# Decay attention and a highway FFN: k and q turned in halves of 64 rows, q loaded eight tokens to a row

## The chip, the cores and the metric

The kernel runs on one core of a Trainium2 chip. The metric is device time in microseconds. Engines are named as the profile names them: PE (matrix multiply, with PEld for its weight loads), DVE, ACT and POOL (elementwise engines), SP (which here only issues transfers). All times below are microseconds unless marked ns.

## The reference

Inputs are q, k and v of shape (4, 8, 768, 64), that is four batches, eight heads, 768 tokens and 64 channels, a decay `lam` per head, and the weights of a highway layer.

```python
for b in range(nb):                       # blocks of 64 tokens
    intra = einsum('bhic,bhjc->bhij', qb, kb) * Dmask      # lam^(i-j), causal
    out   = einsum('bhij,bhjd->bhid', intra, vb)
    out  += einsum('bhid,bhde->bhie', qb * lam_pow, kv_state)
    kv_state = lam_block * kv_state + einsum('bhsd,bhse->bhde', kb * rev_pow, vb)
x = out, heads side by side               # (3072 tokens, 512)
H = relu(x @ w_h);  T = sigmoid(x @ w_t + b_t)
return T * H + (1 - T) * x
```

The kernel computes the same in blocks of 128 tokens with the decay put into q (as lam to the token's number) and into v (as its inverse), so the mask is plain ones and zeros and the state needs no factor.

## The kernel before, in words

The 3072 tokens are cut into 12 steps n of 256 tokens, three to a batch; each step has two blocks b of 128 tokens, one on each half of the 128 partitions. One partition holds two neighbouring tokens (J = 2), so a load of k, q or v is made of runs of 512 bytes. Each step has six loads of 256 KB (`Lk`, `Lq`, `Lv`, each in two halves of four heads); the weights come as four transfers of 512 KB (`W`).

The order of everything is written out by hand in one list, `PLAN`. A token is an operation with its step, the engine after `@` and the PSUM banks after `=`; each engine runs its tokens in the list's order. For a step:

- `CK`, `CQ`, `CV` cast k to bf16, and scale q and v by the decay into bf16 (mostly on POOL).
- `TK`, `TQ` turn k and q on PE, eight transposes of 128x128 each, each into one bank (L204); `EK`, `EQ` copy the two banks to SBUF (128x1024, on ACT or DVE).
- `SS` computes scores of one head parity and, between them, the update of the state kv (L216 and L221; 64x64 tiles of the array). `S` and `U` are the same two apart, for step 0. `KE` copies the state (tile ss).
- `M` multiplies the scores by the mask `tri` on DVE (L255, tile m).
- `I` starts the output o from state times q (L271, 128x128 tiles); `A` adds masked scores times v (L281, 64x64 tiles).
- `D` copies o from PSUM to xT in bf16, the FFN's input (L101 on ACT, L103 on DVE).
- `F` is a block of eight FFN matmuls of 256 columns (L300, result bh for w_h, bt for w_t; the names F.n.u.w carry w as the last number); `H`, `G`, `X` are relu and subtract (tile hm, DVE), sigmoid (ACT, in place) and the gate (tile th, DVE). The last step is done as two groups of 128 columns, 11 and 12.
- `R` turns xT and th back and adds them: 32 matmuls of 64 rows, 128 columns and 64 moving columns, the row halves in turn, into two banks (L347, result bx; for the last step L327 with 128 rows); `E` copies the result to o and `ST` stores it.
- `Z` are matmuls on zeros in the start (bspin, L366); `WC` casts the weights; `B` and `BC` bring the bias into place.

Loads and stores are all issued by SP in the list's order. The transfers share eight semaphores in turn, so one waits for the eighth last.

The lines that the change rewrites most, the turns and the taking of o:

```python
for j in range(J):
    T.transpose(t[:, i, j, :], get(x + "b", n)[:, j, h:h + 2, :], id128)
...
copy(eng, xT[...].rearrange("p n (q j) -> p n j q", j=J),      # writes every second element
     get("o", n, b).rearrange("p n (j q) -> p n j q", j=J))
```

Of the kernel before, what the change touches and what calls it, by code (L numbers as in the profile page):

```python
# [17 lines left out]
Lk.0.0 Lv.0.1 Lv.0.0 Lq.0.0 Lk.0.1 Lq.0.1 Lv.1.1 CK.0.0@POOL Lq.1.0 Z.12=0 TK.0.0=0 Lq.1.1 CV.0.0@DVE Lk.1.0  # L18
CQ.0.0@POOL EK.0.0@DVE Lv.1.0 CV.0.1@DVE CK.0.1@ACT Lk.1.1 Z.11=1 TQ.0.0=1 B=2 EQ.0.0@ACT CQ.0.1@POOL W.0.1 W.0.0
Z.6=0 TQ.0.1=3 TK.0.1=4 EQ.0.1@DVE U.0.0 EK.0.1@ACT W.1.1 S.0.0=56 KE.0.0@DVE S.0.1=01 CQ.1.2@POOL W.1.0 M.0.0.1 Z.1=3  # L20
U.0.1 I.0=34 M.0.1.1 KE.0.1@ACT Lk.2.1 M.0.0.0 A.0.1 M.0.1.0 TQ.1.2=0 Lq.2.1 CV.1.2@DVE CK.1.2@ACT EQ.1.2@ACT Lq.2.0
Z.8=1 TK.1.2=1 A.0.0 EK.1.2@DVE Lk.2.0 D.0.0@DVE Z.3=5 SS.1.1=56 WC.0.0.1@ACT WC.0.0.0@POOL M.1.1.0 KE.1.0@ACT
WC.0.1.0@POOL D.0.1@ACT Lv.2.1 WC.0.1.1@DVE Z.4=0 SS.1.0=01 M.1.1.1 I.1=35 KE.1.1@ACT Lv.2.0 F.0.0.0=4 WC.1.1.0@DVE PT
M.1.0.1 Lk.3.1 F.0.1.0=6 M.1.0.0 WC.1.0.0@POOL WC.1.0.1@ACT Lk.3.0 WC.1.1.1@DVE A.1.1 A.1.0 BC F.0.0.1=1 H.0.1 Lq.3.1
D.1.1@ACT H.0.0 D.1.0@ACT F.0.1.1=0 Lq.3.0 CQ.2.2@POOL F.1.0.0=2 Lv.3.0 G.0.1@ACT CK.2.2@DVE F.1.0.1=6 Lv.3.1
G.0.0@ACT X.0.1@DVE TQ.2.2=5 Lq.4.0 X.0.0@DVE TK.2.2=4 EQ.2.2@ACT CV.2.2@POOL F.1.1.0=3 Lq.4.1 EK.2.2@DVE G.1.0@ACT
H.1.0 SS.2.0=01 Lk.4.1 H.1.1 CK.3.2@POOL SS.2.1=54 Lk.4.0 M.2.0.1 F.1.1.1=2 KE.2.0@ACT M.2.1.0 Lv.4.0 TK.3.2=3 M.2.1.1
CQ.3.2@POOL G.1.1@ACT I.2=15 M.2.0.0 Lv.4.1 A.2.1 X.1.0@DVE A.2.0 Lk.5.0 R.0=40 D.2.0@ACT D.2.1@DVE CV.3.2@POOL
TQ.3.2=6 E.0.0@ACT Lk.5.1 F.2.1.1=1 E.0.1@ACT EQ.3.2@DVE Lq.5.1 EK.3.2@ACT X.1.1@DVE F.2.1.0=5 CQ.4.2@POOL Lq.5.0
R.1=40 H.2.1 SS.3.1=62 Lv.5.0 F.2.0.0=3 CK.4.2@POOL KE.3.0@ACT M.3.1.1 Lv.5.1 E.1.1@ACT M.3.1.0 SS.3.0=52 E.1.0@ACT  # L30
H.2.0 Lq.6.0 TQ.4.2=0 KE.3.1@ACT CV.4.2@POOL M.3.0.1 TK.4.2=6 G.2.1@ACT Lq.6.1 F.2.0.1=4 M.3.0.0 EQ.4.2@ACT EK.4.2@DVE
Lv.6.0 I.3=32 A.3.0 CK.5.2@POOL A.3.1 Lk.6.1 SS.4.1=56 D.3.0@ACT D.3.1@DVE TK.5.2=0 KE.4.0@ACT M.4.1.1 Lk.6.0
F.3.0.0=2 G.2.0@ACT CQ.5.2@POOL EK.5.2@DVE Lv.6.1 SS.4.0=36 H.3.0 F.3.0.1=0 Lq.8.0 M.4.0.0 CV.5.2@POOL M.4.0.1
TQ.5.2=2 Lk.9.0 G.3.0@ACT F.3.1.0=3 X.2.1@DVE Lq.7.0 EQ.5.2@ACT X.2.0@DVE F.3.1.1=6 CQ.6.2@POOL M.4.1.0 Lq.7.1
KE.4.1@ACT I.4=14 H.3.1 G.3.1@ACT R.2=25 Lk.8.1 X.3.0@DVE A.4.0 E.2.1@ACT X.3.1@DVE A.4.1 Lk.7.1 SS.5.0=30 E.2.0@ACT
D.4.0@DVE CK.6.2@POOL SS.5.1=56 D.4.1@ACT Lk.7.0 TQ.6.2=2 M.5.0.0 KE.5.0@ACT CV.6.2@POOL TK.6.2=1 M.5.1.1 Lv.7.0
EQ.6.2@ACT F.4.1.0=4 M.5.0.1 Lv.7.1 EK.6.2@ACT F.4.0.0=3 H.4.1 Lk.8.0 M.5.1.0 I.5=62 SS.6.1=01 H.4.0 Lq.8.1 A.5.0
KE.6.0@ACT M.6.1.0 CQ.7.2@POOL R.3=45 Lv.9.1 A.5.1 M.6.1.1 SS.6.0=30 D.5.0@ACT Lv.8.0 F.4.0.1=1 M.6.0.0 D.5.1@ACT
M.6.0.1 Lk.9.1 TQ.7.2=6 G.4.0@ACT CK.7.2@POOL F.5.0.0=3 Lq.10.1 EQ.7.2@ACT F.4.1.1=2 H.5.0 Lk.10.1 E.3.1@ACT X.4.0@DVE
TK.7.2=0 CV.7.2@POOL G.4.1@ACT I.6=63 ST.0 KE.6.1@DVE F.5.0.1=5 X.4.1@DVE Lv.8.1 F.5.1.0=1 G.5.0@ACT CK.8.2@POOL  # L40
EK.7.2@DVE Lq.9.0 A.6.0 E.3.0@ACT H.5.1 A.6.1 SS.7.1=20 Lq.9.1 D.6.0@ACT D.6.1@DVE TK.8.2=4 M.7.1.1 F.6.1.0=1 Lv.9.0
EK.8.2@ACT X.5.0@DVE CK.9.2@POOL F.6.1.1=6 KE.7.0@DVE Lk.10.0 CQ.8.2@POOL H.6.1 R.4=30 SS.7.0=54 Lk.11.1 E.4.0@ACT
F.5.1.1=1 E.4.1@ACT M.7.0.1 G.6.1@ACT ST.4 M.7.1.0 TK.9.2=3 Lq.10.0 M.7.0.0 TQ.8.2=0 G.5.1@ACT CV.8.2@POOL F.6.0.0=4
EQ.8.2@DVE Lk.11.0 KE.7.1@ACT X.5.1@DVE I.7=25 EK.9.2@ACT Lq.11.0 A.7.0 H.6.0 A.7.1 CQ.9.2@POOL SS.8.0=01 X.6.1@DVE
D.7.1@ACT Lv.10.1 SS.8.1=34 M.8.0.1 D.7.0@ACT F.6.0.1=6 KE.8.0@DVE Lq.11.1 CK.10.2@POOL F.7.0.0=5 M.8.1.0 G.6.0@ACT
M.8.1.1 ST.3 TQ.9.2=1 CV.9.2@POOL H.7.0 F.7.1.0=2 EQ.9.2@ACT Lv.10.0 X.6.0@DVE TK.10.2=3 M.8.0.0 ST.1 I.8=45
EK.10.2@ACT CQ.10.2@POOL H.7.1 SS.9.1=61 A.8.1 KE.9.0@ACT M.9.1.0 A.8.0 R.5=02 M.9.1.1 SS.9.0=36 CK.11.2@POOL
E.5.1@DVE F.7.0.1=1 KE.9.1@ACT M.9.0.1 E.5.0@ACT F.7.1.1=2 D.8.0@DVE D.8.1@ACT ST.5 CQ.11.2@POOL M.9.0.0 G.7.0@ACT
Lv.11.1 TK.11.2=6 Lv.11.0 I.9=04 F.8.1.0=5 EK.11.2@ACT ST.2 X.7.0@DVE TQ.10.2=3 G.7.1@ACT H.8.1 CV.10.2@POOL F.8.0.0=1
EQ.10.2@ACT R.6=65 H.8.0 A.9.1 X.7.1@DVE A.9.0 SS.10.1=31 D.9.0@ACT D.9.1@DVE F.8.1.1=2 E.6.1@ACT M.10.1.1 F.9.1.0=0  # L50
E.6.0@DVE G.8.1@ACT M.10.1.0 ST.6 TQ.11.2=4 CV.11.2@POOL KE.10.0@DVE F.9.1.1=5 EQ.11.2@ACT X.8.1@DVE SS.10.0=16
G.9.1@ACT H.9.1 R.7=32 M.10.0.1 KE.10.1@ACT F.8.0.1=4 X.9.1@DVE E.7.0@ACT M.10.0.0 E.7.1@ACT I.10=06 SS.11.0=53
G.8.0@ACT ST.7 A.10.0 M.11.0.0 A.10.1 SS.11.1=21 D.10.1@ACT X.8.0@DVE F.9.0.0=5 KE.11.0@ACT M.11.1.0 D.10.0@ACT
# [12 lines left out]
def kernel(  # L66
# [13 lines left out]
    C = 128  # L80
# [4 lines left out]
    J = 2  # L85
    N = B * NST
# [12 lines left out]
    def copy(eng, dst, src):  # L99
        if eng == "ACT":  # L100
            A.activation(dst, src, AF.Copy)  # L101
        else:
            ENG[eng].tensor_copy(dst, src)  # L103


    lam_bc = singles.tile([128, H], F32)
    A.dma_start(out=lam_bc, in_=lam.partition_broadcast(128))
    bt_r = singles.tile([KC, 128], F32)
    A.dma_start(out=bt_r, in_=moe_b_t.rearrange("(j p) -> j p", p=128))
    id128 = singles.tile([128, 128], BF16)  # L110
    make_identity(nc, id128)
    blank = singles.tile([128, 512], BF16)
# [53 lines left out]


    SRC = {"k": k, "q": q, "v": v}

    def load(x, n, p, eng):  # L170
        b, c = divmod(n, NST)
        hs = heads(p)
# [246 lines left out]
```

## Time and profile before

| | |
|---|---|
| median of 8 runs | 109.35 (108.67 to 110.16) |
| the profiled execution | 108.67, with a span of 106.8 and a mean PE clock of 0.991 of full speed |
| busy in the span | PE 100.0, DVE 82.4, ACT 71.8, POOL 55.6 |
| first F (L300) starts, last one ends | 22.1, 101.6 |
| moved | 20.98 MB read, 6.29 MB written; SP's queue 88.7% of 16 engines' span |
| eight transposes of 128x128 (L204) | 0.45 on the chain |
| xT<-bo, 128x512 | 750 ns on ACT (16), 728 ns on DVE (8) |
| ss<-kv, 128x512 | 596 ns on ACT (15), 680 ns on DVE (5) |
| qb, vs 128x1024 on POOL | 1902 ns each |

The busy time of PE counts modelled ends of matmuls, which overlap; the time a block takes on PE is read from the start of one block to the start of the next, which the chain of waits shows. Up to 13 us the program waits for its first loads; then the steps follow each other, a few in flight at a time; from about 95 only the FFN of the last steps and the stores are left.

### The profile page before, as it was taken

The numbers are of one execution on the slowest core, as the hardware profiler recorded it, in microseconds if no ns is written. First come the engines' busy times: TensorE is split into PE (matmuls) and PEld (weight loads), VectorE is DVE, ScalarE is ACT, GpSimd is POOL, SyncE is SP. The second block draws the span as 40 slices with busy tenths as digits, with TensorE's granted clock in tenths as the row PEclk, the third lists the DMA queues.
The fourth block names the chain that finished last, engine by engine and source line by source line (L and its number), as shares of the span: only waits on it lengthen the run. The fifth ranks groups of instructions, "written<-read, shape, count | busy, mean of one in ns | idle before, by whom it ended". The sixth has DMA issues, their size and how long they took to land.

```text
span 106.8 us, 4970 instructions
## 1 busy us (share of the span) xinstructions
PE 100.0 (94%) x2190; PEld 80.9 (76%) x2190; DVE 82.4 (77%) x140; ACT 71.8 (67%) x129; POOL 55.6 (52%) x46
## 2 busy tenths in 40 slices
PE   4997999999999999999999999999999999999950
PEld 1343655488987888899889888989898888889930
DVE  1053495879799687999995996999977998858860
ACT  2213244786875678599769776987697797587940
POOL 7028340427889987988368394999870700000000
PEclk9999999999999999999999999999999999999996
DMA  2799999999999999999999999999969335008264
GB/s 36 190 307 291 291 354 386 328 291 262 295 298 295 294 292 288 289 298 289 290 281 302 303 350 299 335 314 333 332 211 339 117 145 196 6 6 327 72 247 146
DMA packets 42701, 27.59 MB, mean 258 GB/s; under 512 B 1588, under 2 KB 38712, under 8 KB 42680
## 3 DMA queue, kind: packets, MB, share of 16 engines
q1 hardware_dynamic: 42528, 27.27, 88.7%
q8 instruction: 17, 0.28, 1.1%
q14 instruction: 4, 0.03, 0.1%
q10 hardware_dynamic: 152, 0.01, 0.1%
HBM read 20.98 MB, written 6.29 MB: 255 GB/s over the span
## 4 chain that ended last, share of the span: by engine, by line
PE 79%; DVE 6%; DMA 5%; issue 2%; POOL 1%; SPq 1%; ACT 1%; POOLq 0%; DVEq 0%
PE bt L300 19%; PE bh L300 18%; PE bs L216 8%; PE bo L281 7%; PE bx L347 6%; PE bqtr L204 6%; DMA qf<-in_q_dram 5%; PE bktr L204 5%; PE bspin L366 5%; PE bo L271 4%; DVE m L255 4%; PE kv L221 2%; POOL qb L190 1%; DVE hm L305 1%; SPq L173 1%
## 5 line engine op out<-in xcount | busy, mean ns | idle before, releaser
L300 PEld LDWEIGHTS <-w_b 128*128 128x128 bf16 x416 | 36.4, 98 | 4.6
L255 DVE TENSOR_TENSOR m<-bs,tri 128x512 bf16<-128x512 f32 x48 | 31.0, 680 | 2.2 <-PE bs L216 1.9
L190 POOL TENSOR_TENSOR qb<-qf,pow_q 128x1024 bf16<-128x1024 f32 (+1 forms) x13 | 23.5, 1811 | 9.3 <-DMA qf<-in_q_dram 9.1
L314 ACT ACTIVATE bt<-bt,bt_col 128x256 f32<-128x256 f32 (+1 forms) x52 | 22.0, 432 | 5.7 <-PE bt L300 2.9
L300 PE MATMUL bh<-xT,w_b 128*128 128x256 bf16 (+1 forms) x208 | 25.0, 265 | 0.0
L300 PE MATMUL bt<-xT,w_b 128*128 128x256 bf16 (+1 forms) x208 | 24.5, 265 | 0.0
L190 POOL TENSOR_TENSOR vs<-vf,pow_v 128x1024 bf16<-128x1024 f32 x10 | 19.0, 1902 | 7.0 <-DMA vf<-in_v_dram 5.8
L305 DVE SCALAR_TENSOR_TENSOR hm<-bh,xT 128x512 bf16<-128x512 f32 (+1 forms) x26 | 16.5, 643 | 3.7 <-PE bh L300 2.1
L318 DVE TENSOR_TENSOR th<-bt,hm 128x512 bf16<-128x512 f32 (+1 forms) x26 | 16.5, 642 | 2.4 <-ACT bt L314 2.3
L101 ACT ACTIVATE xT<-bo 128x512 bf16<-128x512 f32 x16 | 11.6, 750 | 4.5 <-PE bo L281 4.5
L366 PE MATMUL bspin<-blank,id 128*128 128x512 bf16 x45 | 13.1, 440 | 1.4 <-POOL id masks.py:199 1.4
L216 PE MATMUL bs<-qT,kT 64*64 64x128 bf16 x384 | 13.8, 218 | 0.3
L103 POOL CAST kb<-kf 128x1024 bf16<-128x1024 f32 (+1 forms) x10 | 9.9, 994 | 6.1 <-DMA kf<-in_k_dram 5.9
L101 ACT ACTIVATE ss<-kv 128x512 bf16<-128x512 f32 x15 | 8.9, 596 | 6.0 <-PE bs L216 4.7
L216 PEld LDWEIGHTS <-kT 64*64 64x64 bf16 x384 | 10.9, 106 | 2.6 <-issue 1.1
L101 ACT ACTIVATE o<-bx 128x512 f32<-128x512 f32 x19 | 10.4, 596 | 1.4 <-PE bx L347 1.3
L101 ACT ACTIVATE qT<-bqtr 128x1024 bf16<-128x1024 bf16 (+1 forms) x10 | 9.8, 980 | 1.8 <-PE bqtr L204 1.8
L366 PEld LDWEIGHTS <-id 128*128 128x128 bf16 x45 | 4.5, 110 | 7.1 <-issue 2.8
L281 PE MATMUL bo<-m,vs 64*64 64x128 bf16 x384 | 9.3, 219 | 0.5 <-DVE m L255 0.4
L221 PE MATMUL kv<-vs,kb 64*64 64x64 bf16 x320 | 9.1, 196 | 0.0
L281 PEld LDWEIGHTS <-vs 64*64 64x64 bf16 x384 | 6.5, 106 | 2.3 <-issue 1.4
L101 ACT ACTIVATE kT<-bktr 128x1024 bf16<-128x1024 bf16 (+1 forms) x7 | 6.8, 972 | 1.9 <-PE bktr L204 1.9
(50 smaller groups left out, 109.7 us busy)
## 6 DMA issues: line engine op xcount, KB each, us to landing
kf<-in_k_dram SPq DMA_DIRECT2D x24, 256.0 KB, 5.4
vf<-in_v_dram SPq DMA_DIRECT2D x24, 256.0 KB, 5.3
qf<-in_q_dram SPq DMA_DIRECT2D x24, 256.0 KB, 5.5
out_dram<-o SPq DMA_DIRECT2D x11, 512.0 KB, 3.7
w_f<-in_moe_w_h_dram SPq DMA_DIRECT2D x2, 512.0 KB, 6.7
w_f<-in_moe_w_t_dram SPq DMA_DIRECT2D x2, 512.0 KB, 8.6
out_dram<-oh SPq DMA_DIRECT2D x2, 128.0 KB, 2.0
out_dram<-oq SPq DMA_DIRECT2D x1, 256.0 KB
```

The source lines that it names most:

```text
L101: A.activation(dst, src, AF.Copy)
L190: ENG[eng].tensor_tensor(dst, in0=get(src, n)[:, heads(p)].rearrange("p h (j d) -> p h j d", j=J), in1=pw[:, n % NST, heads(p), :, None].t ...
L204: T.transpose(t[:, i, j, :], get(x + "b", n)[:, j, h:h + 2, :], id128)
L216: T.matmul(get("s", n, e, hp // 2)[half(b), hp % 2, j, :], lhsT=get("kT", n)[half(e), hp, j, half(b)], rhs=get("qT", n)[half(e), hp, :, ha ...
L221: T.matmul(kv[half(e), hp, half(e)], lhsT=get("kb", n)[half(b), j, 2 * hp + e, :], rhs=get("vs", n)[half(b), 2 * hp + e, j, :], start=firs ...
L255: V.tensor_tensor(new(("m", n, e, u), [128, 2, J, C]), in0=get("s", n, e, u), in1=tri[:, None].to_broadcast([128, 2, J, C]), op=ALU.mult)
L281: T.matmul(get("o", n, b)[half(e), hp, :], lhsT=get("vs", n)[half(b), 2 * hp + e, j, :], rhs=get("m", n, e, u)[half(b), hp % 2, j, :], sta ...
L300: T.matmul(t[:, r, :], lhsT=w_b[w][:, kc, (2 * u + r) * 128:(2 * u + r + 1) * 128], rhs=get("xT", *g)[:, kc, :], start=(kc == 0), stop=(kc ...
L305: V.scalar_tensor_tensor(new(("hm", g, u), [128, 2, z * C], tag=f"hm{z}"), in0=get("h", g, u), scalar=0.0, in1=get("xT", *g)[:, 2 * u:2 * ...
L314: A.activation(dst[:, r, :], src[:, r, :], AF.Sigmoid, bias=bt_col[:, 2 * u + r:2 * u + r + 1])
L318: ENG[eng].tensor_tensor(new(("th", g), [128, NP, z * C], tag=f"th{z}")[:, 2 * u:2 * u + 2, :], in0=get("tt", g, u), in1=get("hm", g, u), ...
L366: T.matmul(t, lhsT=id128, rhs=blank, start=True, stop=True)
```

## The change

- **k and q are turned in halves of 64 rows.** One token `T` stands for `TK` and `TQ`. It makes 32 transposes of 64 rows with 64 moving columns; the halves (the two blocks of 128 tokens) take turns and go to two banks, each of which holds k and q of one block. `ET` copies one bank (two per step, 128x1024 each) into one tile that holds both blocks.
- **q is loaded eight tokens to a row.** A partition holds one group of eight tokens of one head pair, and each of the two loads of a step brings one head of every pair, in runs of 2 KB. Its powers of lam need constants of their own: a second small load of `lam` on ACT, three more index tiles and some small DVE operations. In the turned tile the four head pairs of a token lie side by side, so scores and `I` read q with a step of four elements. The mask's columns and the order of tokens in o follow.
- **D** reads o from PSUM with a step (of 16 elements) and writes xT in order.
- **Transfers wait for the fifth last.** From the 15th on, a transfer on SP's queue, loads and stores alike, has a wait for the one five before it.
- **The list `PLAN` is another one**: the order of all tokens and the engines and banks of many differ. At the start, k's first half is followed by five loads of q and only then by the rest of k, then v, then w_h; w_t's two parts come later and apart.

```diff
-    lam_bc = singles.tile([128, H], F32)
-    A.dma_start(out=lam_bc, in_=lam.partition_broadcast(128))
+    lam_bc = singles.tile([128, H + 2], F32)
+    A.dma_start(out=lam_bc[:, 0:H], in_=lam.partition_broadcast(128))
+    A.dma_start(out=lam_bc[:, H:H + 2], in_=lam.rearrange("(h x) -> h x", x=2)[None].to_broadcast([32, NP, 2]))
...
-    tri = singles.tile([128, J, J, C // J], F32)
+    tri = singles.tile([128, J, Q, C // Q], F32)
...
+    issued = []
+    def dma(dst, src, eng=None):
+        i = (eng or nc.sync).dma_start(out=dst, in_=src)
+        if len(issued) >= 14:
+            tc.add_manual_dep(i.ins, issued[-5].ins.name, ...)
+        issued.append(i)

     def load(x, n, p, eng):
         b, c = divmod(n, NST)
+        ts = slice(c * 2 * C, (c + 1) * 2 * C)
+        if x == "q":
+            dst = new(("qf", n), [128, 2, Q * D], F32)
+            dma(dst[:, p], q[b, :, ts, :].rearrange("(h x) (o j) d -> x o h (j d)", x=2, j=Q)[p])
+            return
...
+    def cast_q(n, p, eng):
+        js = slice(0, Q) if p == 2 else slice(4 * p, 4 * p + 4)
+        z = js.stop - js.start
+        ENG[eng].tensor_tensor(new(("qb", n), [128, Q, 2, D])[:, js].rearrange("p j x d -> p x j d"),
+                               in0=get("qf", n).rearrange("p x (j d) -> p x j d", j=Q)[:, :, js],
+                               in1=pow_q[:, n % NST, :, js, None].to_broadcast([128, 2, z, D]), op=ALU.mult)
...
-    def trans(x, n, p, bk):
+    def trans(xs, n, p, bk):
         hs = heads(p)
-        t = bank((x + "tr", n, p), bk[0], [128, (hs.stop - hs.start) // 2, J, C], BF16)
-        for i, h in enumerate(range(hs.start, hs.stop, 2)):
-            for j in range(J):
-                T.transpose(t[:, i, j, :], get(x + "b", n)[:, j, h:h + 2, :], id128)
+        for b, i in enumerate(bk):
+            bank(("tr", n, p, b), i, [128, 2, (hs.stop - hs.start) // 2 * C // 2 * J], BF16)
+        if "k" in xs:
+            t = [get("tr", n, p, b)[:, 0].rearrange("p (h j i) -> p h j i", j=J, i=C // 2) for b in range(2)]
+            for i, h in enumerate(range(hs.start, hs.stop, 2)):
+                for j in range(J):
+                    for b in range(2):
+                        T.transpose(t[b][:, i, j, :], get("kb", n)[half(b), j, h:h + 2, :], id128[half(b), half(b)])
+        if "q" in xs:
+            t = [get("tr", n, p, b)[:, 1].rearrange("p (j i) -> p j i", i=C // 2) for b in range(2)]
+            for i in range(Q if p == 2 else Q // 2):
+                for b in range(2):
+                    T.transpose(t[b][:, i, :], get("qb", n)[half(b), i + (4 if p == 1 else 0)], id128[half(b), half(b)])
+
+    def evac_t(n, p, b, eng):
+        es = slice(0, 512) if p == 2 else slice(256 * p, 256 * p + 256)
+        copy(eng, new(("T", n), [128, 2, 2, 512], tag="kT")[:, b, :, es], get("tr", n, p, b))
+
+    def kT(n, b, hp):
+        return get("T", n)[:, b, 0].rearrange("p (h j i) -> p h j i", h=NP, j=J)[:, hp]
+
+    def qT(n, b, hp):
+        return get("T", n)[:, b, 1].rearrange("p (i h) -> p i h", h=NP)[:, :, hp]

     def score(n, e, hp, j, b):
-        T.matmul(get("s", n, e, hp // 2)[half(b), hp % 2, j, :], lhsT=get("kT", n)[half(e), hp, j, half(b)],
-                 rhs=get("qT", n)[half(e), hp, :, half(b)], start=True, stop=True)
+        T.matmul(get("s", n, e, hp // 2)[half(b), hp % 2, j, :], lhsT=kT(n, b, hp)[half(e), j, :],
+                 rhs=qT(n, b, hp)[half(e)], start=True, stop=True)
...
-                             rhs=get("qT", n)[:, hp, :, half(b)],
+                             rhs=qT(n, b, hp),
...
     def take(n, b, eng):
-        copy(eng, new(("xT", *g), ...)[...].rearrange("p n (q j) -> p n j q", j=J),
-             get("o", n, b).rearrange("p n (j q) -> p n j q", j=J))
+        copy(eng, new(("xT", *g), ...)[...].rearrange("p n (q j) -> p n q j", j=Q),
+             get("o", n, b).rearrange("p n (j q) -> p n q j", j=Q))
```

The first two lines of the list before and the first two after:

```diff
-Lk.0.0 Lv.0.1 Lv.0.0 Lq.0.0 Lk.0.1 Lq.0.1 Lv.1.1 CK.0.0@POOL Lq.1.0 Z.12=0 TK.0.0=0 Lq.1.1 CV.0.0@DVE Lk.1.0
-CQ.0.0@POOL EK.0.0@DVE Lv.1.0 CV.0.1@DVE CK.0.1@ACT Lk.1.1 Z.11=1 TQ.0.0=1 B=2 EQ.0.0@ACT CQ.0.1@POOL W.0.1 W.0.0
+Lk.0.1 Lq.0.0 Lq.2.1 Lq.1.1 Lq.1.0 Lq.0.1 Lk.0.0 Lk.1.1 Lk.1.0 Z.8=0 B=0 CK.0.1@ACT BC PT TK.0.1=12 Lv.0.0
+Lv.0.1 CQ.1.2@POOL CQ.0.0@DVE Lv.1.0 CK.0.0@DVE Lv.1.1 Z.13=0 TQ.0.0=34 CQ.0.1@POOL TK.0.0 Lk.2.0 ET.0.0.1@DVE
```

## The prediction

> **What bounds the kernel now.** I read the share of busy time by engine first, then the chain that ended last in order of time, then the waits, then the engines by stage, then the transfers.
>
> ```profile
> PE 100.0 (94%) x2190; PEld 80.9 (76%) x2190; DVE 82.4 (77%) x140; ACT 71.8 (67%) x129; POOL 55.6 (52%) x46
> PEclk9999999999999999999999999999999999999996
> GB/s 36 190 307 291 291 354 386 328 291 262 295 298 295 294 292 288 289 298 289 290 281 302 303 350 299 335 314 333 332 211 339 117 145 196 6 6 327 72 247 146
> ```
>
> PE is busy 94% at full clock. The rate of the transfers is near 290 GB/s while they are all loads of k, q and v, and 386 where the weights pass (2 KB to a row instead of 512 B). A busy PE need not be a PE that issues without a gap, so the chain has to show it:
>
> ```profile
> 22.25 1.75 PE bh L300 x16
> ...
> 54.07 0.57 PE bx L347 x32
> ...
> 56.41 0.45 PE bqtr L204 x8
> 56.85 0.87 PE bh L300 x8
> ...
> 61.02 0.57 PE bo L281 x32
> ...
> 62.03 0.55 PE bktr L204 x8
> ...
> 93.79 1.04 PE bx L347 x64
> 94.83 0.98 PE bh L300 x8
> ```
>
> Columns: start, duration, work, count. From the first FFN block (22.1) to the last (101.6) the chain is almost all PE, block after block. Eight turns of 128 rows cost 0.45, or 0.55 straight after work of another tile shape. A block of 8 FFN matmuls costs 0.87 or 0.98 in the same way. So a change of shape costs about 0.1 (0.094 between single starts). In the bx row, 32 matmuls of 64 rows by 128 columns with 64 moving columns, the two row halves in turn, cost 0.57 with the change of shape; 64 cost 1.04, so 32 more are 0.47.
>
> ```profile
> PE bo L281 <- DVE m L255: 0.4, 2, 0.3
> ```
>
> This is PE's longest wait of its own for another engine between the start and the last turns. Adding up the blocks of PE's order from F.0.0.0 (44 F of 0.87 and 8 of 0.45, 20 groups of turns of 0.45, 11 R and 16 SS of 0.47, 4 SS of 0.24, 22 A of 0.235, I's 68 matmuls of 0.056, 47 changes of shape at 0.094) gives 78.0 to the end of the last F; the trace takes 79.6. So PE's own order is the bound there, and waits are 1.6.
>
> ```profile
> 40.00:50.00 10.00, 10.00 (x284) 8.81 (x281) 9.40 (x16) 8.11 (x17) 8.51 (x6) 1.00 1.11 291
> 70.00:80.00 10.00, 10.00 (x222) 9.12 (x222) 9.31 (x16) 7.87 (x14) 9.00 (x6) 1.00 0.96 300
> ```
>
> Columns after the stretch: sum, then busy PE, weight loads, DVE, ACT, POOL, clock, DMA share, GB/s. DVE is next at 93 to 94%: little is free there. The start, up to 22.1, is another regime, of transfers and the first casts:
>
> ```profile
> 5.50 0.61 POOL L103 CAST kb<-kf 128x512 bf16<-128x512 f32 x1 [2.83 <-DMA kf<-in_k_dram]
> 19.18 1.17 POOL L103 CAST w_b<-w_f 128x512 bf16<-128x512 f32 x2 [4.59 <-DMA w_f<-in_moe_w_h_dram]
> ```
>
> **The turns.** A step's k and q cost 2 x 0.446 = 0.89 (TK, TQ). The T token that replaces them issues 32 turns of 64 rows in alternating halves into two banks, the form of the bx row: 0.47. Ten steps are turned after F.0.0.0: 10 x 0.42 = 4.2 less, all on PE's path. But T has a shape of its own: TK and TQ often stood beside F, free of a change. In the new PE order I count 59 changes of shape from F.0.0.0 on against 47: 12 x 0.094 = 1.1 more. Net 3.1 less. Number and size of the evacuations stay (two of 128x1024 a step, 0.68 on DVE or 1.03 on ACT), as do the casts.
>
> A rule of the Trainium skill speaks against this. "TensorE: Matmul & The Clock Gate", section "Wait — 56ns, not 53.3ns?", says that matmuls never start closer than about 25 ns, however few columns they move; 32 would take an estimated 0.80, the turns would save 0.9 in all and the changes of shape eat it. The bx row has 0.47 / 32 = 14.7 ns per matmul, below that floor, so the row decides.
>
> **q's new order.** Scores and the inter part now read q with a step of four elements (8 bytes) as the moving operand. No matmul of the trace moves a stepped operand. Bounds: nothing, as in rows bs and bo (56 ns for 128 columns, 8 in 0.45); or half rate: 80 inter matmuls x 0.056 = 4.5, and 24 blocks of 16 scores, four tiles at once, 4 x 0.056 each = 5.4; together 9.9. A gain is excluded, as the same elements move. I take nothing: the contiguous rows are PE work of the same size, and the nearest stepped access, DVE's xT cast that writes every second bf16, costs 728 against 680 ns in order, 7%.
>
> The skill's "SBUF — State Buffer", section "Door 1: The DMA port swizzle", bears on it: two hits on each 16-byte line keep full rate, and 8 bytes gives just two. No run so far shows it.
>
> **D.** ACT's xT copy writes with a step in 750 ns; ss, the same size in order, takes 596. Reading 64 bytes apart from PSUM is in no row: between 154 ns less and, at half rate, about 0.5 more for each of 24 (DVE's copies of bx take 418 for 256 elements and 681 for 512, so 512 cost 0.53 beyond the fixed part). I take ACT's 596 and DVE's 680, as the data read are whole 4-byte elements. That frees 13 x 0.154 = 2.0 on ACT and brings the end nothing: the blocks that PE has between A and the first F of the same step (R, T or F of earlier steps) cover it. What it costs if the cover goes is the second rival.
>
> **Transfers.** q in 2 KB runs: 0.90 a transfer at 290 GB/s, 0.68 at 386; 24 x 0.22 = 5.3 of transfer time saved, between 0 and that. In the middle it is worth nothing on PE's path, which hardly waits. Each transfer from the 15th on waits for the fifth last, where eight were let out before. SP carries nothing but transfers: behind a waiting one stand the next loads and, from ST.0 on, stores; POOL's and ACT's casts wait for the loads, the five o buffers for the stores. Five loads of 0.90 hold 4.5 of data, and a store of 512 KB lands in 3.7, of which 1.4 is data, so some 2.3 are delay and 2.2 of data stay queued: I take 0. The other end is a pipe that runs dry for a store at each of the four places where loads stand behind one, 4 x 1.4 on the transfers, of which PE sees only what the prefetched steps do not cover.
>
> **The start.** Both orders spin PE, 45 against 47 times. New loads before F.0.0.0: nine of k and v, five of q, then w_h. From the first landing (5.45): 8 x 0.90 + 5 x 0.68 + 2 x 1.36 = 13.3, plus 1.1 by which the old w_h landed later than the same sum: 19.9; two POOL casts of 0.61, 21.1. If 2 KB brings q nothing: 22.2. PE's own way: v's second half is the 11th transfer, 5.45 + 5 x 0.90 + 5 x 0.68 = 13.4, or 14.5 with the 1.1: 13.9; its scaling on POOL 1.31, 15.2; then U, T, Z, I, A, U, A, Z, SS, Z, SS, I by their rows, 6.4: 21.6. The added constants (small ops of 0.15 to 0.25, a third ACT transfer of 0.45) lie before the first q. F.0.0.0 at 21.7 against 22.1: 0.4 less, from 1.5 less to 1.5 more. Next, w_t's last part is the 24th transfer, 19.9 + 7.5 = 27.4, cast 28.0; PE reaches F.0.0.1 at 21.7 + 6.3 = 28.0. POOL's scaling of q for step 2 ends at 21.1 + 1.9 = 23.0, PE is there at 22.6. I take 0.5 more (0 to 1.5).
>
> **DVE.** It does 68 between 22 and 100, now in 75 rather than 78: 91% instead of 87%. I add 0.4 of waits (from 1.0 less, if the old ones vanish, to 1.5).
>
> **Sum.** -4.2 + 1.1 - 0.4 + 0.5 + 0.4 = -2.6. The profiled execution took 108.67 (span 106.8 and 1.9 around it), so 106.1 and a span of 104.2; the median of the runs, 109.35, lies 0.7 above that execution, so 106.7. About 0.5% is what this measurement can tell from no change.
>
> **The rivals.**
> 1. *PE moves stepped q at less than full rate.* Place: bs and bo's first matmuls, all on PE's path. It decides from 2.6 / 9.9, a quarter of the bound: 128 columns in 71 ns instead of 56. At the full price 106.7 + 9.9 = 116.6; at half 111.6. For it: no row shows the access. Against: DVE's stepped write costs only 7%. Chance 0.15.
> 2. *DVE becomes the bound.* With 11 D on DVE and half-rate reads from PSUM, 11 x 0.5 = 5.5 more brings it to 73 in 75; with its order's gaps PE waits some 3 to 5: 109.7 to 111.5. For it: 93 to 94% already. Against: ACT's price is in the writing. Chance 0.07.
> 3. *Supply eats it.* q in 2 KB is no faster, five in flight leave holes: F.0.0.0 at 23.5 and w_t 1 later, 2.6 to 3 lost: 109.3 to 109.7. For it: the early stage has no slack. Against: 386 GB/s where runs are long. Chance 0.10.
>
> **How the numbers follow.** Forecast 0.68, its own range 103.7 (-4.2 + 1.1 - 1.5 - 1.0 = -5.6) to 108.6 (start 1.5 late: 1.9 more). Then the rivals. To hold eight in ten the range reaches through rivals 3 and 2 and to half of rival 1's price: 103.7 to 111.0, with about 0.1 above it and some below. Faster: the forecast and a small part of rival 3, 0.70. Same: most of rival 3, 0.08. Slower: rivals 1 and 2, 0.22.
>
> **What would show it.** The turns in blocks of 32 with 0.47 (0.57 after another shape); if such a block takes 0.8, the first step is wrong. Eight inter matmuls still 0.45, and single 128-column starts 56 ns apart; 71 or more is rival 1. ACT's xT near 600 ns; above 900 is rival 2, with DVE over 95% in each stage and waits of PE on m or hm. The first bh at 21 to 22.5, w_t's cast before 28.5; later is rival 3. The last PE block about 2.5 earlier than 103. A time above 108.8 would make the prediction wrong.

## The result, and the profile after

The changed kernel takes 121.8 us, the median of 11 runs (120.86 to 122.3); the kernel before took 109.26 beside it. The ratio is 1.1144 (95% interval 1.1114 to 1.1174): 12.5 us slower, outside the range. The profiled execution has a span of 120.1 at a mean PE clock of 0.996. Here and below a median is of all executions of a kernel, while a ratio compares the fast ones alone (those within 1.5% of the fastest of the same kernel), so the two can differ.

First the busy time by engine and, from the chain that ended last, its shares by engine and by line.

```profile
PE 112.3 (94%) x2384; PEld 87.4 (73%) x2384; DVE 85.0 (71%) x145; ACT 69.3 (58%) x130; POOL 56.4 (47%) x47
...
PE 90%; DMA 4%; ACT 2%; DVE 1%; issue 1%; ACTq 0%
```

PE is as busy in share as before (94%), but of a span that is 13.3 longer, and its busy time grew by 12.3. All other engines are busy for a smaller share of the span. So it is not a wait that ate the gain: PE itself works longer. The costliest groups, with shapes kept apart (columns: busy time, mean ns of one, then the idle time before and what ended it), say at which instructions (the last row is the turns of k):

```profile
L258 PE MATMUL bs<-kT 64*64 64x128 bf16 x384 | 23.4, 289 | 0.0
L313 PE MATMUL bo<-kT,ss 128*128 128x128 bf16 x80 | 11.2, 292 | 0.0
L103 DVE CAST xT<-bo 128x512 bf16<-128x512 f32 x11 | 7.6, 687 | 4.4 <-PE bo L323 4.4
L101 ACT ACTIVATE xT<-bo 128x512 bf16<-128x512 f32 x13 | 7.5, 595 | 3.6 <-PE bo L323 3.5
L239 PE MATMUL btr<-id,kb 64*128 64x64 bf16 x192 | 5.1, 193 | 0.8 <-ACT kb L101 0.8
```

Scores (bs) and o's first matmuls (bo from ss) are the two groups that read q. The same two before:

```profile
L216 PE MATMUL bs<-qT,kT 64*64 64x128 bf16 x384 | 13.8, 218 | 0.3
L271 PE MATMUL bo<-qT,ss 128*128 128x128 bf16 x80 | 6.4, 219 | 0.0
```

They took 218 and 219 ns each; now they take 289 and 292. The mean ns of a matmul is the time from its start to its end, not its share of PE, as the next ones start before it ends. The share is read from starts: from the first start to the eighth, eight of o's first matmuls take 391 ns before and 793 ns after, that is one every 56 ns and one every 113. A block of 16 scores with 16 state updates lasts 0.57 from its start to that of the next block in the runs with q in order below, and 1.03 here. The same columns take nearly twice the time. The two rows of xT are as the prediction had them (595 and 687 ns), and 16 turns of k and 16 of q are 217 and 207 ns from first start to last, so T's 32 are done in 0.47.

The waits (time waited in all, how often, the longest) fit that:

```profile
POOL qb L220 <- DMA qf<-in_q_dram: 18.1, 3, 10.6
ACT ss L101 <- PE bs L258: 12.9, 9, 2.8
DVE m L297 <- PE bs L258: 10.8, 13, 2.0
```

ACT and DVE now wait for PE's scores; POOL runs ahead of the loads. And the start, in the timeline (start, length, work; in brackets the idle time before and what ended it):

```profile
6.42 0.21 ACT L142 ACTIVATE ln_bc<-lam_bc 128x10 f32<-128x10 f32 x1 [2.40 <-DMA lam_bc<-in_lam_dram]
6.78 0.23 PE L402 MATMUL bbt<-id_f,bt_r 4*128 4x4 f32 x1 [1.76 <-DMA bt_r<-in_moe_b_t_dram]
8.18 5.45 PE L408 MATMUL bspin<-blank,id 128*128 128x512 bf16 x13
9.81 1.83 DVE L220 TENSOR_TENSOR qb<-qf,pow_q 128x512 bf16<-128x512 f32 x1 [2.17 <-issue]
11.56 1.26 DVE L103 CAST kb<-kf 128x512 bf16<-128x512 f32 x1
```

The second load of lam delays the powers to 6.4 (5.07 before). PE stands idle for bt_r, and of the 13 spins that follow one starts every 0.427, where from 14.9 on one starts every 0.216. The granted clock of this execution is recorded only from 13.2 on; in k1 below, which has the same start, it is 0.52 from 8 to 11, and the spins start 0.427 apart there too. Step 0's first scaling of q needs both of its loads, and the second of them is the fifth q load in the list: it lands at 9.73, and DVE starts at 9.81. This scaling and the cast of k behind it then take 1.83 and 1.26 while POOL scales q beside them. The first F starts at 26.6, not at 21.7.

### The profile page after: what moved, and what is told of

Read it like the earlier page. It is cut to its first block, busy times and chain, and to the rows that moved or that the text cites. A ratio compares the mean times of both kernels' runs of the same rounds, so it can differ in the third digit from the quotient of the medians.

```text
span 120.1 us, 5371 instructions
## 1 busy us (share of the span) xinstructions
PE 112.3 (94%) x2384; PEld 87.4 (73%) x2384; DVE 85.0 (71%) x145; ACT 69.3 (58%) x130; POOL 56.4 (47%) x47
## 4 chain that ended last, share of the span: by engine, by line
PE 90%; DMA 4%; ACT 2%; DVE 1%; issue 1%; ACTq 0%
PE bt L342 19%; PE bh L342 18%; PE bs L258 16%; PE bspin L408 10%; PE bo L313 8%; PE bo L323 6%; PE bx L389 5%; DMA lam_bc<-in_lam_dram 4%; PE btr L239 3%; PE btr L244 3%; PE kv L263 2%; ACT oh L101 1%; ACT kb L101 0%; ACTq L108 0%; DVE th L360 0%
## 5 line engine op out<-in xcount | busy, mean ns | idle before, releaser
L356 ACT ACTIVATE bt<-bt,bt_col 128x256 f32<-128x256 f32 (+1 forms) x52 | 22.1, 433 | 8.2 <-PE bt L342 6.0
L226 POOL TENSOR_TENSOR vs<-vf,pow_v 128x1024 bf16<-128x1024 f32 (+1 forms) x12 | 22.0, 1830 | 9.6 <-DMA vf<-in_v_dram 5.0
L258 PE MATMUL bs<-kT 64*64 64x128 bf16 x384 | 23.4, 289 | 0.0
L101 ACT ACTIVATE ss<-kv 128x512 bf16<-128x512 f32 x20 | 11.9, 595 | 16.1 <-PE bs L258 12.9
L258 PEld LDWEIGHTS <-kT 64*64 64x64 bf16 x384 | 18.4, 119 | 3.4 <-issue 2.8
L101 ACT ACTIVATE kT<-btr 128x1024 bf16<-128x1024 bf16 (+1 forms) x15 | 14.2, 965 | 10.8 <-PE btr L244 10.8
L347 DVE SCALAR_TENSOR_TENSOR hm<-bh,xT 128x512 bf16<-128x512 f32 (+1 forms) x26 | 16.6, 644 | 3.2 <-PE bh L342 2.2
L263 PE MATMUL kv<-vs,kb 64*64 64x64 bf16 x320 | 12.9, 201 | 0.0
L263 PEld LDWEIGHTS <-kb 64*64 64x64 bf16 x320 | 10.9, 107 | 0.4 <-issue 0.4
L313 PE MATMUL bo<-kT,ss 128*128 128x128 bf16 x80 | 11.2, 292 | 0.0
L103 POOL CAST kb<-kf 128x1024 bf16<-128x1024 f32 x9 | 9.3, 1037 | 3.0 <-DMA kf<-in_k_dram 2.1
L103 DVE CAST xT<-bo 128x512 bf16<-128x512 f32 x11 | 7.6, 687 | 4.4 <-PE bo L323 4.4
L101 ACT ACTIVATE xT<-bo 128x512 bf16<-128x512 f32 x13 | 7.5, 595 | 3.6 <-PE bo L323 3.5
```

The costliest lines, as they stand in the source:

```text
L226: ENG[eng].tensor_tensor(new(("vs", n), [128, H, J, D])[:, heads(p)], in0=get("vf", n)[:, heads(p)].rearrange("p h (j d) -> p h j d", j=J) ...
L258: T.matmul(get("s", n, e, hp // 2)[half(b), hp % 2, j, :], lhsT=kT(n, b, hp)[half(e), j, :], rhs=qT(n, b, hp)[half(e)], start=True, stop=True)
L263: T.matmul(kv[half(e), hp, half(e)], lhsT=get("kb", n)[half(b), j, 2 * hp + e, :], rhs=get("vs", n)[half(b), 2 * hp + e, j, :], start=firs ...
L313: T.matmul(get("o", n, b)[:, hp, :], lhsT=get("ss", n, b)[:, hp, :], rhs=qT(n, b, hp), start=hp == 0, stop=False, skip_group_check=True)
L347: V.scalar_tensor_tensor(new(("hm", g, u), [128, 2, z * C], tag=f"hm{z}"), in0=get("h", g, u), scalar=0.0, in1=get("xT", *g)[:, 2 * u:2 * ...
L356: A.activation(dst[:, r, :], src[:, r, :], AF.Sigmoid, bias=bt_col[:, 2 * u + r:2 * u + r + 1])
```

## The experiments

Each kernel is a short edit of the changed kernel unless it says "before"; line numbers in its profile are its own. Starts of single matmuls are read from the trace of each run.

### What does the step in q cost: 2, 4, 8 and 16 bytes

Four kernels leave everything in place and change only which columns of the turned q PE reads, and so which tokens and heads meet.

```diff
 def qT(n, b, hp):                                              # after: step of 4 elements, 8 bytes
-    return T[:, b, 1].rearrange("p (i h) -> p i h", h=NP)[:, :, hp]
+    return T[:, b, 1, hp * C:(hp + 1) * C]                     # e1: in order
+    return T[:, b, 1].rearrange("p (s i h) -> p s i h", s=2, h=2)[:, hp // 2, :, hp % 2]   # e2: 4 bytes
+    return T[:, b].rearrange("p x f -> p (x f)").rearrange("p (i h) -> p i h", h=8)[:, :, hp]  # e4: 16 bytes
 # e3: scores in order as in e1, o's first matmuls as after
```

> The changed kernel, but scores and the inter part move 128 columns of the turned q that lie side by side, so they work on other tokens than they should; everything else stays. Theory A (PE moves an operand with a step of 8 bytes at half rate): the eight inter matmuls go back from 0.79 to 0.39 within the block, a block of 16 scores and 16 state updates from 1.03 to 0.57, and as 16 to 20 such blocks and 68 to 80 inter matmuls lie on PE's path, 12 to 14 of the 12.5 are gone: 107.5 to 109.8. Rival B (the new order and the fuller DVE make PE wait) and rival C (transfers that wait for the fifth last starve the casts): PE's blocks are long because of waits, and the time stays above 119.

> As the kernel with q in order, but with a step of two elements (4 bytes) instead of four; the columns are again other tokens' than they should be. If any step halves the rate: inter block 0.79, time 121 to 123. If the price grows with the bytes that a step skips: inter block 0.39 to 0.6, time 108 to 115.

> The changed kernel, but only the scores move q's columns side by side (other tokens' than they should be); the inter part keeps the step of 8 bytes. Theory A: the inter block stays at 0.79, blocks of scores go back to 0.57; of the price 80 x 0.056 = 4.5 stays: 112 to 114. By the bound of the prediction, four score tiles at once, the scores would give back only 5.4: 116.4.

> As the kernel with q in order, but with a step of eight elements (16 bytes), which reaches over k's part of the tile, so the columns are other data than they should be. If any step halves the rate: inter block 0.79, time 121 to 123. If the price grows with the bytes skipped: inter block 1.2 to 1.6, time 130 to 140.

Measured: e1 110.28 (ratio to before 1.0056, 1.0005 to 1.0108), 0.5 above what was expected; single executions of e2 110.13, e3 112.86 and e4 154.02, the last 14 above its range. The rows of o's first matmuls in e2, then e3, then e4 (there with the scores' row):

```profile
L313 PE MATMUL bo<-kT,ss 128*128 128x128 bf16 x80 | 6.6, 219 | 0.0
```

```profile
L313 PE MATMUL bo<-kT,ss 128*128 128x128 bf16 x80 | 11.2, 292 | 0.0
```

```profile
L258 PE MATMUL bs<-kT 64*64 64x128 bf16 x384 | 42.9, 401 | 0.0
L313 PE MATMUL bo<-kT,ss 128*128 128x128 bf16 x80 | 20.1, 403 | 0.0
```

By starts, eight of these matmuls take 391 ns in order, 405 to 418 with a step of 4 bytes, 793 with 8 and 1570 with 16: per 128 columns 56, 58, 113 and 224 ns. So 4 bytes cost next to nothing, 8 halve PE's rate and 16 quarter it. All of it is bf16, so whether bytes or elements count is not shown. e1 against after is 11.5 us by the medians, 11.9 by the ratios; e3 (one execution), which keeps the step in o's first matmuls alone, stands 2.6 above e1, so the scores are the larger part.

### Does a kernel that computes the same gain it back

k1 keeps the loads, the turns, the order and the fifth-last wait, and puts q in order where it is copied out of PSUM, in two copies instead of one (lines shortened):

```diff
 def evac_t(n, p, b, eng):
-    copy(eng, T[:, b, :, es], tr)
+    copy(eng, T[:, b, 0, es], tr[:, 0])
+    copy(eng, T[:, b, 1].rearrange("p (h i) -> p h i", h=NP)[:, :, cs], tr[:, 1].rearrange("p (i h) -> p h i", h=NP))
 def qT(n, b, hp):
+    return T[:, b, 1].rearrange("p (h i) -> p h i", h=NP)[:, hp]
```

> The changed kernel, computing the same, with its loads, turns, order and fifth-last wait as they are, but with q put in order where it is copied out of PSUM: each copy of a turned bank is made in two instructions, k's half as before, q's half read with a step of four elements and written in order, so that scores and bo's first matmuls read neighbouring columns. Theory (the step in q on PE costs some 11.5): eight of bo's first matmuls within 391 ns, DMA share as in the changed kernel without the step, the first F at 24.8 to 25.5, 110.3 and up to 1.5 more for the second instruction of 24 copies (ACT and DVE some 0.25 us each time): 110 to 112. Rival (something else in the order or the loads takes a large part of the loss): over 114.

111.75 (110.72 to 111.99), ratio 1.023 (1.018 to 1.028). The groups:

```profile
L261 PE MATMUL bs<-kT 64*64 64x128 bf16 x384 | 13.8, 218 | 0.6 <-issue 0.6
L316 PE MATMUL bo<-kT,ss 128*128 128x128 bf16 x80 | 6.5, 219 | 0.0
```

One edit, in which PE reads neighbouring columns, takes 10.0 us off a kernel that computes the same. The step is the cause of the loss. But 2.3% above the kernel before is not 2.4% below it; the rest is followed further on. Part of it is k1's own: it stands 1.7% above e1 by the ratios, and e1 has neither the step nor the second copies.

### Two layouts that avoided the step and lost the gain on the way

i1 turns the partitions of q round, head pair first and token group second, so that q is read in runs of 16 neighbours; j1 (and j2) puts row half, token group, head pair, for a step of 4 bytes, with four transfers of 128 KB a step instead of two of 256 KB, and without the fifth-last wait. i2 is i1 with the start of the list rewritten, i3 is i2 without the fifth-last wait, and j2 is j1 with the start rewritten.

```diff
-dma(dst[:, p], q[b, :, ts, :].rearrange("(h x) (o j) d -> x o h (j d)", x=2, j=Q)[p])
+dma(dst[:, p], q[b, :, ts, :].rearrange("(h x) (o j) d -> x h o (j d)", x=2, j=Q)[p])                     # i1
+for y in range(2):                                                                                       # j1
+    dma(dst[half(p), y], q[b, :, ts, :].rearrange("(r h x) (o j) d -> r x o h (j d)", r=2, x=2, j=Q)[p][y])
```

> The changed kernel, computing the same, with q's partitions laid out head pair first and token group second: each load of q is still made of runs of 2 KB, a turned half then holds two head pairs of all 256 tokens, and scores and bo's first matmuls read q in runs of 16 neighbouring columns (32 bytes) that lie 128 bytes apart. Theory (PE pays for the distance between neighbouring elements, not for the jumps between runs): eight of bo's first matmuls within 391 ns, 110.3 as in the run with columns in order (109.8 to 111.0), the first F near 24.8. Rival (every run's jump costs as a step does, one column in 16): 391 + 8 x 8 x 0.9 = 450 ns, 111 to 112. Rival (the price is for any pattern of three levels): 793 ns, 121.8.

> The same layout, and the start rewritten: all loads of steps 0 and 1 and w_h ahead of step 2, spins in one run without the bias transpose between them, casts of k on ACT, w_t's two parts one after the other, and the second F of step 0 and step 1's masked scores ahead of the turns of step 2. Theory (e1 and e2 were level with the kernel before because their first F was 2.6 late and DVE's waits cost 1.4): the first F at 20.5 to 21.5 and 80 to 81.5 from there to the last matmul: 105.5 to 107.5. Rival (supply sets the middle whatever the start: turns of step 2 then wait for loads by what the start gained): 108.5 to 110.

> The same without the wait for the fifth last transfer. Theory (the wait costs nothing where runs of 2 KB keep the pipe full): the same within 0.6. Rival (five in flight starve the start): 1 to 2 faster, with T's wait for step 2 shorter.

> The changed kernel, computing the same, with q's rows laid out so that scores and bo's first matmuls read q with a step of two elements (4 bytes) and every q transfer's outer dimension is 32: row half, token group, head pair, in four transfers of 128 KB a step instead of two of 256 KB, and without the wait for the fifth last. Theory (i1 was slow because its q transfers, outer dimension 4, kept only 4.2 of 16 DMA engines busy; PE's price is for the step in bytes): q's 2 KB packets again fill the queue (over 300 GB/s from 8 to 30 us), eight of bo's first matmuls within 402 to 418 ns as in e2, the first F at 24 to 25.5, 109.5 to 111. Rival (a transfer to 64 partitions reaches only half of the memory and is slow too): under 250 GB/s while q is loaded, the first F after 26, 112 or more.

> The same with the start rewritten (all loads of steps 0 and 1 and w_h ahead of step 2, spins in one run, casts of k on ACT, the bias transpose after step 0's attention, the second F of step 0 and step 1's masked scores ahead of the turns of step 2, w_t's two parts one after the other). Theory (the changed order without the step stands level with the kernel before only because its first F comes 2.6 later): the first F at 20.5 to 22, 106 to 108. Rival (supply sets the middle whatever the start; what the start gains, the turns of step 2 and w_t wait for): 108.5 to 110.5.

i1 151.24, i2 149.33, i3 147.07: the expected times of i1 and i2 missed by 40 us and more, and i3, expected level with i2 or 1 to 2 below it, stands 2.3 below. PE did what the theory said (eight of o's first matmuls within 391 ns, a block of scores 0.57). The chain is another:

```profile
DMA 55%; PE 23%; SPq 14%; issue 2%; ACT 1%; POOL 1%; DVE 1%; POOLq 0%
...
DMA  2124659994948374853857685627636699330355
```

The first line is the chain's share by engine, the second the DMA share of 40 slices. While i1's first five q loads are under way, for some 12 us, the packets of 2 KB keep 4.2 DMA engines busy at any time (the sum of their times over the time that passes); in the changed kernel up to 16.6. A q load of i1 has 4 as its outermost count (head pairs), that of the changed kernel 32 (token groups). "DMA: Bandwidth & Descriptors" in the Trainium skill, section "Why a DMA increments its semaphore by 16 and not by 1", says that a transfer is dealt out over the largest number of engines, up to 16, that divides the slowest dimension of both its sides; with 4 that is four, and the 4.2 agree.

j1 119.17, j2 117.79: that was mended (up to 16 engines with 2 KB packets), yet both missed the times of their theories by 8 and more; j1's time lies where its rival, slow loads, had it. SP's own line in j2's timeline, then the same line in the changed kernel's:

```profile
1.30 3.33 SPq L191 DMA_DIRECT2D qf<-in_q_dram  x4
```

```profile
1.31 3.58 SPq L190 DMA_DIRECT2D qf<-in_q_dram  x5
```

In such a row one q transfer holds SP for 0.83 with 128 KB there and for 0.72 with 256 KB here; a single one later in the list holds it for 0.54 in either kernel (at 31.43 in j2, at 14.31 in the changed one), while i1's five of 256 KB, slow to land, hold it for 7.54. So the time goes by the transfer and by what is ahead of it more than by its bytes, and a step needs four instead of two. From 6 to 22 us the DMA engines are as full in j2 as in the changed kernel (share 1.08 and 1.09), but they move 275 GB/s instead of 366. PE waits up to 1.8 us at turns, scores and state updates, and after the longest wait in the middle the granted clock is 0.5 from 55.7 to 59.2, with FFN matmuls 213 ns apart instead of 109. Which part each of these has was not separated.

### The parts of the change alone

d1 is the kernel before with D alone changed. f3 is the changed kernel's order and turns with q loaded two tokens to a row as before, hence in order; f4 is f3 with another start. g1 is the kernel before, in its own order, with one T in place of TK and TQ for steps 1 to 11. h1 is the changed kernel without the fifth-last wait.

> The kernel before with D alone changed: o is read from PSUM with a step and xT is written in order. xT on ACT 0.60 instead of 0.75, on DVE 0.69 instead of 0.73, as in the changed kernel; the time stays within 0.5% of before (108.8 to 109.9), as PE does not wait for ACT. If ACT were on the path: 108 or less.

> The changed kernel with one part undone: q is loaded two tokens to a row and scaled and turned as k is, so its columns lie side by side; the 64-row turns, D, the wait for the fifth last and the new order stay. Theory A (the step is the loss): as with q in order, 109.3 to 111.5, the first F at 24 to 25.5. Theory D (the load of eight tokens with its constants is what makes the start late): the first F back at 22 to 23 and 107 to 108.5. If the new order or the wait for the fifth last were the loss: above 115.

> As the one before, with another start: loads in the order k, q, v of step 0, then step 1, then the weights; all of step 0's q on POOL and k on ACT, v on DVE; 16 spins at once so that PE does not stand still and cool; the bias later; fewer spins later. If cold spins and DVE beside POOL make the start late: the first F at 21.5 to 22.5, 2 to 3 less than with the two-token load alone: 106.8 to 108.5. If the weights' transfers set it: the first F still at 24.5, 109.5 to 111.

> The kernel before with the turns of steps 1 to 11 alone done in halves of 64 rows: T stands at the place of the later of TQ and TK, two banks, each with one block's k and q; the rest of the order, the loads and D stay. PE's blocks sum to 76.2 instead of 78.9 from the first F (63 changes of shape instead of 47): 106.2 to 107.5 if nothing else becomes late. If the evacuations now come too late (both after the later turn), the gain is eaten: 108.5 to 110.

> The changed kernel without the wait for the fifth last transfer. Theory (the step of eight bytes is the cost, the wait costs nothing): 121.8 within 0.8, the first F at 26.6 within 0.5, bo's eight first matmuls 793 ns as before. Rival (the wait starves the pipe): 118 to 120, and the gain lies in DMA waits of POOL and PE.

- d1 109.07, ratio 0.9999 (0.9972 to 1.0026): xT 597 ns on ACT and 682 on DVE (medians), and no time gained, as the prediction said of D.
- h1 121.54 (121.21 to 122.04): the wait costs nothing in this order.
- f3 112.44, ratio 1.0279 (1.0217 to 1.0341); f4 111.57, 1.0249 (1.021 to 1.0288). Without the step by another road, and level with k1. Neither met a range: f3's first F came at 22.6, as its theory D had it, but its time stands 0.9 above theory A's; f4's first F came at 20.7, and its time stands 0.6 above its upper range. With runs of 512 bytes the DMA engines are near full through the middle (share 0.97 to 1.00 in f4 from 22 to 80), and f4's earlier first F was paid back: the turns of step 2 waited 2.0, and others 0.8 to 1.3.
- g1 118.86, ratio 1.088 (1.0831 to 1.0928): both expectations missed. PE's busy time is what before's is, but PE is 85% busy, and the chain is made of waits too:

```profile
PE 50%; DVE 20%; ACT 11%; issue 8%; DMA 5%; POOL 1%; SPq 1%; DVEq 0%; ACTq 0%; POOLq 0%
```

One T wants k and q cast and two banks free at one time, where TK and TQ each wanted one of each, and PE's turns now wait for DVE's masks and gates (1.5 and 1.5 in all). So in the order made for the single turns they cost 8.8%. That the order that came with them is what they need is an argument; no run changes g1's order alone.

### Where the other 5 us went: the start and what follows it

k2 is k1 with the start rewritten (all loads of steps 0 and 1, then w_h, then step 2; casts of k on ACT; the bias transpose later; fewer spins; step 0's second F and step 1's A ahead of step 2's turns) and without the fifth-last wait; k3 is k2 with that wait; k4 is k1 with most of the named causes of its late start undone: 16 spins in one run without the bias transpose between them, step 0's two q loads side by side, k's first casts not on DVE, and w_h ahead of step 2. It keeps the second load of lam.

```diff
-Lk.0.1 Lq.0.0 Lq.2.1 Lq.1.1 Lq.1.0 Lq.0.1 Lk.0.0 ... Z.8=0 B=0 CK.0.1@ACT BC ... CK.0.0@DVE ... Z.13=0 ... Z.6=0 SS.1.1 ... Z.4=1 SS.1.0
+Lk.0.1 Lq.0.0 Lq.0.1 Lk.0.0 Lq.1.1 Lq.1.0 ... Z.16=0 CK.0.1@POOL ... CK.0.0@ACT ... W.0.1 W.0.0 Z.10=0 ... B=1 ... BC ... Z.2=0 SS.1.1 ... Z.1=1 SS.1.0   (k4)
```

> The same with the rewritten start of the run before (loads of steps 0 and 1 and w_h ahead of step 2, bias transpose after step 0's attention, second F of step 0 and step 1's masked scores ahead of the turns of step 2, w_t's parts one after the other) and without the wait for the fifth last. Theory (the order is only level with the kernel before because its start is 2.6 late): the first F at 20.5 to 22, 106 to 108.5. Rival (the supply sets it: turns of step 2, w_t or kv wait for what the start gained): 109 to 111.

> The run before (q in order, start rewritten) with the wait for the fifth last transfer put back, to see what that wait does where the first loads and weights are let out in one run. Theory (the supply limits the stage after the first F, and the wait neither helps nor hurts by more than 0.6, as in the changed kernel): 111.5 to 113. Rival 1 (with up to eight let out, transfers share the engines and the needed ones land late; five at a time land sooner): 109 to 111 and a narrower spread than 109 to 114. Rival 2 (five starve the pipe): above 113.

> q in order as in k1, the changed kernel's order from step 2 on and its fifth-last wait, and only the causes named for the late start undone: no bias transpose among the first spins (16 spins in one run, then 10), k's first casts on POOL and ACT instead of ACT and DVE, step 0's q and k and then w_h moved ahead of step 2's loads, 9 fewer spins between step 0 and step 1, the last w_h cast on ACT. Theory (those causes hold the first F 2.5 late, and the middle does not lose it again): the first F at 21.5 to 23, 108.3 to 110.2. Rival (supply gives it back, as in k2): the first F as early, 110.5 to 112.

k2 112.52 (109.07 to 114.39), ratio 1.0112 (1.0058 to 1.0166); k3 110.1 (108.48 to 112.33), ratio 1.0007 (0.9954 to 1.0061); k4 110.57 (107.74 to 112.9). k2 missed both its ranges, k3 lies in that of its rival 1, and k4 at the low end of its rival's. The runs of these three spread by 3.9 to 5.3 us, where those of the kernel before spread by 1.6 beside k3 and k4 and, with one outlier, by 3.8 beside k1 and k2, so the order among the three stays open. Reading one profiled execution of each (108.67 before, 110.72 for k1, 108.87 for k3, 109.87 for k4) for four things, by starts of matmuls on PE (a stall is the part of a gap over what the columns and a change of shape take, where it is over 60 ns):

| us | first F | first F to last matmul | of this stalls | the rest | last matmul |
|---|---|---|---|---|---|
| before | 22.1 | 81.0 | 1.3 | 79.7 | 103.1 |
| k1 | 24.6 | 80.0 | 3.4 | 76.6 | 104.6 |
| k3 | 21.5 | 81.4 | 4.7 | 76.6 | 102.9 |
| k4 | 20.3 | 83.5 | 6.8 | 76.8 | 103.9 |

In these executions an earlier first F is given back in part or nearly whole, as stalls: 3.1 earlier in k3 against k1 ends as 1.7, and 4.2 earlier in k4 ends as 0.7. k4's profile is not of its fastest execution, which took 107.74 and has no trace. k3's PE timeline shows its two largest:

```profile
25.70 0.72 PE L261 MATMUL bs<-kT 64*64 64x128 bf16 x23 [1.16 <-DVE kT L103]
...
29.98 1.92 PE L345 MATMUL bt<-xT,w_b 128*128 128x256 bf16 x16 [0.71 <-DVE w_b L103]
```

and k4's:

```profile
22.39 0.41 PE L239 MATMUL btr<-id,kb 64*128 64x64 bf16 x16 [1.01 <-ACT kb L101]
...
28.62 1.92 PE L345 MATMUL bt<-xT,w_b 128*128 128x256 bf16 x16 [0.74 <-DVE w_b L103]
```

They are step 2's turns and copies and w_t's cast, but what stands behind them differs. In k4 it is transfers: ACT's cast of k waits for its load until 21.28, and w_t's last part lands at 27.73, with its cast at 27.75. In k3 it is not. There step 2's k and q are cast by 22.83 and its turns start at 23.89 without a wait; but k3's list has the scores of step 2 right behind the turns, where k1 has two A and an F between, so PE waits for the copies (24.62 to 25.64). And w_t's last part lands at 26.31, while DVE comes to cast it at 28.55 and takes 1.37, where the kernel before has 0.42 for the same cast. So part of what k3 loses lies in its own order, and whether a better one would keep the gain was not tried. Nor is it shown that the fifth-last wait matters in k3's order: the intervals of k2's and k3's ratios just touch.

No version is shown to beat the kernel before; k3 is level with it, and k4's one execution of 107.74, below all 17 of the kernel before beside it, is too little to say more.

## Why the prediction was wrong, point by point

**The step that failed: q's step taken at nothing.** The prediction saw that no row showed the access, bounded it from 0 to 9.9, and took 0 because the contiguous rows are PE work of the same size and because DVE pays only 7% for a stepped write. In its place the runs show half rate: 793 ns instead of 391 for eight matmuls, 10.0 to 11.9 us of the kernel's time. A stepped write of DVE is no neighbour of a stepped read of PE. The rule of the Trainium skill that stood beside it, "SBUF — State Buffer", section "Door 1: The DMA port swizzle", says that two hits on a line of 16 bytes keep full rate, which a step of 8 bytes gives. For PE's moving operand these runs contradict it: 4 hits a line (405 to 418 ns) are near full rate, 2 hits (793) are half, 1 hit (1570) a quarter. Rival 1 named this mechanism, its place and its sign, at a chance of 0.15.

**Its upper bound was mis-sized too.** 9.9 came from 80 x 0.056 and 24 blocks of 16 scores "four tiles at once". But in 22 of the 24 blocks the 16 scores all read one row half of the array, and the state updates have the other; only two scores run at once. The prediction's own row for such a block, 0.47, already said so: it is 16 x 0.057 / 2. So the price of half rate is 80 x 0.057 = 4.6 and 24 x 16 x 0.057 / 2 = 10.9, 15.5 in all, and a block's 0.57 to 1.03 is that 16 x 0.057 / 2. e4, at a quarter of the rate, bears the size out: three times 15.5 is 46.5, and it stands 43.7 above e1. Of the 15.5 the time shows 10.0 (against k1) to 11.9 (against e1); the rest lies over waits which the kernel has without the step (DVE is 15% of k1's chain, 1% of the changed kernel's) and over spins in the start.

**The turns and the changes of shape were right.** -4.2 and +1.1 make -3.1; without stalls PE's way from the first F on went from 79.7 to 76.6. A T takes 0.47, as the bx row promised, again 14.7 ns a matmul.

**The start was wrong by 2.9, apart from the step.** Predicted 0.4 earlier; in k1 the first F is 2.5 later, and in the changed kernel, where step 0 and step 1 pay for the stepped reads as well, 4.5 later. The prediction timed the start by the transfers and by PE's rows at full clock. It said that the added constants "lie before the first q", but the second load of lam held ACT's first cast. It did not see that PE, idle for bt_r, would spin at half the rate (k4, with 16 spins in one run, has one every 0.216 from 4.8 on), nor that step 0's first q scaling needs the fifth q load. And it had no term for DVE's operations on step 0's path, which took 1.83 and 1.26, nor for the last cast of w_h, which k1's first F waits for:

```profile
22.57 1.93 DVE L103 CAST w_b<-w_f 128x512 bf16<-128x512 f32 x1
24.56 1.05 PE L345 MATMUL bh<-xT,w_b 128*128 128x256 bf16 x8 [0.56 <-DVE w_b L103]
```

POOL scales v beside this cast; in the kernel before, with POOL idle, one of this size takes 0.42. k4, with most of this undone, starts F at 20.3: its step 0 q is there by 7.83, and DVE scales it in 0.69. The share of each cause was not measured.

**The waits after it were under-priced.** w_t 0.5 and DVE 0.4 were added; k1 has 2.1 more stalls than before, and its second copies may be part of them (DVE is busy 96% of the time from 22 to 60, 90% in e1). With the start this closes the sum between the two profiled executions: -3.1 + 2.5 + 2.1 = +1.5, and the last matmul goes from 103.1 to 104.6. Another 0.6 lies behind the last matmul. k1's profile is of its fastest execution: by the medians it stands 2.6 above the kernel before.

**Rival 2 is shown wrong** (ACT's xT 595, DVE 71% busy). **Rival 3** was right in sign for what is left once the step is out: e1, f3 and k1 end 0.6 to 2.8% above the kernel before. Its mechanism does not hold for k1: the transfers are faster with q in 2 KB runs (356 GB/s from 6 to 22, where the kernel before moves 293 from 8 to 14), and what the first F waits for last is DVE's cast, not a transfer. The fifth-last wait cost nothing where it was taken out alone (h1, with the step in place).

## What to carry to other kernels

When a change alters how PE reads an operand, look at the step in bytes of its innermost dimension: here, in bf16, 4 bytes cost next to nothing and 8 already halve the rate. If a layout forces such a step, take it in the copy out of PSUM, which cost 1.5 us here by the medians and 1.9 by the ratios (k1 against e1), where PE paid 10 and more. When no row shows an access, take no comfort from another engine's row, and count what really runs at once before writing an upper bound. And a saving at the start of a kernel is worth only what the stages behind it, their transfers and their order, can take up.

## What the runs showed of the hardware

- PE's moving operand in SBUF, bf16: 56, 58, 113 and 224 ns per 128 columns for steps of 2, 4, 8 and 16 bytes. Runs of 16 neighbours with jumps of 128 bytes between them cost nothing (391 ns for eight).
- Loads whose outermost count is 4 kept 4.2 DMA engines busy (i1), those with 32 up to 16.6 (the changed kernel).
- In a row of q transfers SP took 0.72 for each of 256 KB and 0.83 for each of 128 KB, and 0.54 for a single one of either size; a load split in two holds the issuing queue twice.
- DVE's 128x512 scaling of q took 1.83 and its cast of w_h 1.93 where POOL was already scaling beside it. The same scaling took 0.69 in k4, where DVE started ahead of POOL, and the cast 0.42 in the kernel before with POOL idle.
